# Whole expert tiles as pairs of 64-row half products, ordered by a one-word ScalarE copy

## The chip, the cores and the metric

The kernel runs on one core of a Trainium2 chip. The metric is device time in microseconds (us) of one execution. The core's engines run instruction streams of their own and meet only at semaphores: TensorE (PE: matmuls, and PEld: its weight loads), VectorE (DVE), ScalarE (ACT), GpSimd (POOL) and SyncE (SP), which issues most DMAs. SBUF is the on-chip memory with 128 partitions; PSUM holds TensorE's sums, in eight banks of 512 32-bit numbers a partition.

## The reference

Two stages. First an attention without softmax, for 8 batches of 2496 tokens, 256 channels and 64 key channels; then a mixture of 8 experts, of which each token takes the best one.

```python
scores = np.matmul(z, z.transpose(0, 2, 1)) / S
attn = np.maximum(scores, 0.0) ** 2
x = (u * np.matmul(attn, v)).reshape(N, D)            # N = 19968, D = 256

logits = x @ w_gate + modality_bias[modality_id]
e_idx = np.argmax(logits, axis=1)                     # E = 8
gate_w = softmax(logits)[arange(N), e_idx]
for e in range(E):
    mask = e_idx == e
    h = np.maximum(x[mask] @ w1[e], 0.0)              # F = 1024
    out[mask] = gate_w[mask, None] * (h @ w2[e])
```

## The kernel before, in words

All products use fp32r operands. To keep the precision, each operand is split into a high part and a low part, and a product is the sum of three: high by high, high by low, low by high.

The attention stage works through steps of two key tiles (2 x 128 rows) against 512 (in the last chunk 448) queries. Its contraction over 64 channels, and its weighing by key rows, are laid out as products on 64 rows of the array: rows 0-63 and rows 64-127 hold two different ones, which run side by side and write to different banks (`scores`, L279; `weigh`, L334). ACT squares and rounds, DVE makes low parts. At the end of a chunk the output is turned into rows of tokens by transposes on TensorE (`make_rows` L412; for the very last chunk `make_last_rows` L394) and multiplied by u (`take_rows`, `take_last_rows` L403); DVE makes the gate's logits (L434), and POOL scatters the tokens into one DRAM list per expert (L547).

The expert stage takes tiles of T = 512 tokens of one expert. Four "early" tiles, t = -4 to -1, belong to the expert with the most tokens and start before routing is complete; in between their steps the rest of the logits, the routing and the plan of all later tiles are made (lists `between[n][f]`, run after step f of the n-th tile). Tiles 0 to 34 follow the plan, so 39 tiles are whole. What is left over goes through `run_quarter` and, under conditions read at run time, further tiles.

For one whole tile `run_tile` goes through f = 0 to 7, one slice of 128 of the 1024 hidden channels each:

- `up(t, f)`: six products of 128 x 128 weights and 512 tokens add into one bank of `ps_h` (four banks, tag "h"): 2 halves of the contraction over 256 channels, 3 terms each. ACT then writes `hh` = relu of the bank, rounded (L1009), and DVE the low part `hl` (L1010).
- `down(t, f - 2, ...)` for each of J = 4 groups of 128 tokens: one product of `hh` with the high and low parts of w2 side by side (512 columns, L1018) and one of `hl` with the high part (256 columns, L1019). They add into four banks of `ps_o`, one for each group, over all eight f.
- After the last step `finish` scales by the gate: ACT takes one half of the bank (L1033), DVE adds the other (L1035), and POOL scatters the rows to the output with an indirect DMA (L1037).

Beside the products, for the next tile: `part_weights_high` / `part_weights_low` split its weights into high parts (ACT, L831) and low parts (DVE, L835), in four quarters at f = 2 to 5; `turn_blocks` transposes its tokens (DVE, L853) at f = 6, and `part_high` (ACT, L860) and `part_low` (DVE, L865) split them at f = 7. `fetch_weights(t + 2)` issues two DMAs of 1 MB on SP's queue (L811, L815) at the start of a tile, into one of three weight buffers; `prefetch` issues the DMAs of tokens (L792).

In this stage the order on PE, ACT, DVE, POOL and SP is the order in which the program issues the instructions (`manual_schedule`); every engine works its queue in order.

## Time and profile before

| | |
|---|---|
| median of 3 runs | 2243.7 us (2242.93 to 2245.5) |
| profiled execution, its own time | 2245.74 us |
| its span, first to last instruction | 2243.9 us |
| mean granted TensorE clock | 0.997 |
| PE busy | 2221.6 us, 99% of the span |
| DVE busy | 1804.4 us, 80% |
| ACT busy | 1573.0 us, 70% |
| up products of 512 columns (L1005) | 1872 of 128 x 128 weights |
| down products, 512 / 256 columns (L1018 / L1019) | 1256 / 1256 |

An engine's busy time counts its own instructions, without waits. In the timelines below, each row is one instruction or a run of like ones: start, length, engine, line, operation, output and inputs by their names in the program, rows x columns of the weights, shape of the moving operand, count, and in brackets the idle time before it with what ended it. TensorE's products overlap: the next one starts before the last has ended, so the cost of one in a stream is the distance from start to start. A product's end is modelled from its start.

### The profile page before, as it was taken

The numbers are of one execution on the slowest core, as the hardware profiler recorded it, in microseconds if no ns is written. First come the engines' busy times: TensorE is split into PE (matmuls) and PEld (weight loads), VectorE is DVE, ScalarE is ACT, GpSimd is POOL, SyncE is SP. The second block draws the span as 40 slices with busy tenths as digits, with TensorE's granted clock in tenths as the row PEclk, the third lists the DMA queues.
The fourth block names the chain that finished last, engine by engine and source line by source line (L and its number), as shares of the span: only waits on it lengthen the run. The fifth ranks groups of instructions, "written<-read, shape, count | busy, mean of one in ns | idle before, by whom it ended". The sixth has DMA issues, their size and how long they took to land.

```text
span 2243.9 us, 44470 instructions
## 1 busy us (share of the span) xinstructions
PE 2221.6 (99%) x16874; PEld 2020.7 (90%) x16874; DVE 1804.4 (80%) x4552; ACT 1573.0 (70%) x1917; POOL 366.3 (16%) x349
## 2 busy tenths in 40 slices
PE   9999999999999999999999999999999999999996
PEld 7889999999999999999999888888888888888885
DVE  7889989989989989989989998666666666666663
ACT  7888888888888888888888873455555555555452
POOL 0000220220210210220220422211111111111111
PEclk9999999999999999999999999999999999999998
DMA  5222223222012112112111122754545454545440
GB/s 184 111 70 101 83 89 110 79 74 79 32 59 75 35 57 76 35 56 75 39 45 40 51 88 62 187 158 126 157 128 155 127 155 130 152 134 149 135 140 23
DMA packets 199602, 216.64 MB, mean 97 GB/s; under 512 B 118448, under 2 KB 166064, under 8 KB 194512
## 3 DMA queue, kind: packets, MB, share of 16 engines
q1 hardware_dynamic: 184288, 172.49, 26.3%
q0 software_dynamic: 15088, 41.21, 5.0%
q8 instruction: 134, 2.20, 0.4%
q14 instruction: 92, 0.75, 0.1%
HBM read 168.23 MB, written 62.19 MB: 103 GB/s over the span
## 4 chain that ended last, share of the span: by engine, by line
PE 59%; issue 25%; DMA 9%; POOL 3%; DVE 3%; ACT 1%; POOLq 0%; DVEq 0%; ACTq 0%
PE acc L334 44%; PE s L279 12%; DMA out_dram<-y,ids 9%; POOL out_dram L1037 3%; DVE spare L434 1%; PE ph L1005 1%; PE po L412 1%; PE po L1018 1%; DVE al L318 1%; PE po L1019 0%; DVE vl L249 0%; POOLq L1037 0%; PE warm L886 0%; DVE ah L309 0%; DVE x L382 0%
## 5 line engine op out<-in xcount | busy, mean ns | idle before, releaser
L287 ACT ACTIVATE r<-s 128x1024 f32<-128x1024 f32 (+1 forms) x395 | 397.8, 1007 | 184.5 <-PE s L279 182.7
L318 DVE TENSOR_TENSOR al<-r,ah 128x1024 fp32r<-128x1024 f32 (+1 forms) x359 | 429.8, 1197 | 84.1 <-ACT ah L309 68.9
L334 PE MATMUL acc<-ah,vh 64*128 64x512 f32 (+1 forms) x3120 | 492.8, 383 | 1.0 <-DVE ah L301 1.0
L334 PE MATMUL acc<-ah,vl 64*128 64x512 f32 (+1 forms) x3120 | 487.0, 382 | 0.0
L334 PE MATMUL acc<-al,vh 64*128 64x512 f32 (+1 forms) x3120 | 483.8, 381 | 0.0
L434 DVE SCALAR_TENSOR_TENSOR spare<-x,wgb 128x256 f32<-128x256 f32 x1280 | 462.4, 421 | 1.0
L1009 ACT ACTIVATE hh<-ph 128x512 fp32r<-128x512 f32 x312 | 186.6, 598 | 388.2 <-PE ph L1005 348.1
L1018 PE MATMUL po<-w,hh 128*128 128x512 f32 x1256 | 450.0, 394 | 0.0
L1005 PE MATMUL ph<-xh,w 128*128 128x512 f32 x1248 | 430.1, 395 | 1.4 <-DVE x L382 1.4
L293 ACT ACTIVATE r<-r 128x1024 f32<-128x1024 f32 (+1 forms) x399 | 415.6, 1042 | 3.5
L334 PEld LDWEIGHTS acc<-ah,vh 64*128 64x128 f32 x3120 | 383.3, 184 | 17.7 <-ACT x L378 1.7
L334 PEld LDWEIGHTS acc<-al,vh 64*128 64x128 f32 x3120 | 383.0, 184 | 14.6
L334 PEld LDWEIGHTS acc<-ah,vl 64*128 64x128 f32 x3120 | 381.3, 184 | 15.0 <-DVE vl L249 0.2
L1010 DVE SCALAR_TENSOR_TENSOR hl<-ph,hh 128x512 fp32r<-128x512 f32 x312 | 215.7, 691 | 219.5 <-ACT hh L1009 191.8
L279 PE MATMUL s<-zm 64*128 64x512 f32 (+1 forms) x2400 | 388.8, 386 | 0.8 <-ACT r L287 0.3
L547 POOL DMA_INDIRECT xs<-x,sloti x160 | 206.5, 1291 | 1016.2 <-DVE x L545 971.9
L1019 PE MATMUL po<-w,hl 128*128 128x256 f32 x1256 | 351.5, 280 | 0.2 <-DVE hl L1010 0.2
L279 PEld LDWEIGHTS s<-zm 64*128 64x128 f32 x2400 | 292.6, 185 | 12.3 <-ACT r L287 0.8
L309 ACT CAST ah<-r 128x1024 fp32r<-128x1024 f32 (+1 forms) x283 | 288.1, 1018 | 0.0
L1005 PEld LDWEIGHTS ph<-xh,w 128*128 128x128 f32 x1248 | 234.2, 188 | 57.6 <-DVE x L382 1.8
L1018 PEld LDWEIGHTS po<-w,hh 128*128 128x128 f32 x1256 | 235.7, 188 | 55.4
L1037 POOL DMA_INDIRECT out_dram<-y,ids x157 | 152.8, 974 | 693.7 <-DVE y L1035 659.2
(155 smaller groups left out, 1979.4 us busy)
## 6 DMA issues: line engine op xcount, KB each, us to landing
w<-w1s SPq DMA_DIRECT2D x37, 1024.0 KB
w<-w2s SPq DMA_DIRECT2D x37, 1024.0 KB
xg<-xs SPq DMA_DIRECT2D x156, 128.0 KB
vr<-in_v_dram SPq DMA_DIRECT2D x32, 512.0 KB
ut<-in_u_dram SPq DMA_DIRECT2D x32, 512.0 KB
zr<-in_zt_dram SPq DMA_DIRECT2D x40, 256.0 KB
w1s<-in_moe_w_dram SPq DMA_DIRECT2D x16, 512.0 KB
w2s<-in_moe_w_dram SPq DMA_DIRECT2D x8, 1024.0 KB
```

What stands on the lines that cost most here:

```text
L279: nc.tensor.matmul(out=s[t][:, :w], lhsT=lhs, rhs=mv[halves[t], ql, :w], start=n == 0, stop=n == 2)
L287: nc.scalar.activation(out=r[:, :, :w], in_=both[:, :, :w], func=AF.Relu, scale=INV)
L293: nc.scalar.square(out=a[:, :, :w], in_=a[:, :, :w])
L309: copy(out=ah[:, :, :w], in_=st_a[g][:, :, :w])
L318: nc.vector.tensor_tensor(out=al[:, :, :w], in0=a[:, :, :w], in1=ah[:, :, :w].bitcast(F32), op=ALU.subtract)
L334: nc.tensor.matmul(out=acc[b, c][r][dh][:, :w], lhsT=V[b, k // J][y][halves[r], k % J, dh * P:(dh + 1) * P], rhs=x[halves[r], k % 2, :w], ...
L434: nc.vector.scalar_tensor_tensor(out=spare[:, k % 2, :], in0=x[:, j, 0:D], scalar=1.0, in1=wgb[:, e, :], op0=ALU.mult, op1=ALU.mult, accum ...
L1005: nc.tensor.matmul(out=ph, lhsT=lhs, rhs=rhs[:, k, :], start=n == 0, stop=n == 3 * KD - 1)
L1010: nc.vector.scalar_tensor_tensor(out=hl, in0=ph, scalar=0.0, in1=hh.bitcast(F32), op0=ALU.max, op1=ALU.subtract)
L1018: nc.tensor.matmul(out=po[j], lhsT=hh[:, s], rhs=both, start=f == 0, stop=False, skip_group_check=True)
L1019: nc.tensor.matmul(out=po[j][:, 0:D], lhsT=hl[:, s], rhs=w[:, 0, :], start=False, stop=f == KF - 1, skip_group_check=True)
L1037: nc.gpsimd.indirect_dma_start(out=out, out_offset=bass.IndirectOffsetOnAxis(ap=ids[:, j:j + 1], axis=0), in_=y, in_offset=None, bounds_ch ...
```

## The change

Whole tiles are run by a new `run_whole`. `run_tile` stays for what is under conditions.

- A product over all 128 rows becomes two half products: rows 0-63 and rows 64-127 of the same operands. They are issued in pairs: rows 0-63 for one slice beside rows 64-127 for its neighbour (direction d = 0), and in a later pass the other way round (d = 1). In `up_half` the two slices are two slices of hidden channels with a bank of `ps_h` each; in `down_half` they are two groups of 128 tokens with a bank of `ps_o` each.
- Thus each bank gets the sums of one row half first and those of the other later. `product` notes which half wrote a bank last (`writer`). Where it was the other half, the product is made to wait for the ScalarE copy held in `ended["act"]`. `change` issues such a copy, of one word of SBUF, which waits for the last product issued before it, and makes it the one held.
- Order in a tile: `UPS` gives for each of eight steps the pair of slices and the direction of the up pass; `DOWNS` the slices and the direction of a down pass behind it. Two down passes of a tile, `last_but_one` (slices 4 to 7, d = 1) and `last` (slices 6 and 7, d = 0, and `finish`), go to the list `behind` and are run in the first two steps of the next tile.
- The quarters of the next tile's weights are split at steps 0 (two), 3 and 7, `turn_blocks` moves to step 5, `part_high` and `part_low` to step 6, and `fetch_weights(t + 2)` to the end of step 1.
- The last chunk's rows of the attention stage are turned by `make_rows` (16 half transposes in place of 8 whole ones), into two banks of `ps_o`, at step 0 of the first tile.

```diff
@@ -993,6 +975,13 @@
     for n in range(1, NW):
         weight_tiles(wp, n)
 
+    def rectify(ph, nt):
+        hh = mp.tile([P, T], F32R, tag="hh", bufs=4, name="hh")[:, 0:nt]
+        hl = mp.tile([P, T], F32R, tag="hl", bufs=4, name="hl")[:, 0:nt]
+        nc.scalar.activation(out=hh, in_=ph, func=AF.Relu)
+        nc.vector.scalar_tensor_tensor(out=hl, in0=ph, scalar=0.0, in1=hh.bitcast(F32), op0=ALU.max, op1=ALU.subtract)
+        return hh, hl
+
     def up(t, f):
         _, xh, xl = TL[t]
         w = weights_of(t)[0]
@@ -1004,11 +993,53 @@
             for lhs, rhs in ((wh, xh), (wh, xl), (wl, xh)):
                 nc.tensor.matmul(out=ph, lhsT=lhs, rhs=rhs[:, k, :], start=n == 0, stop=n == 3 * KD - 1)
                 n += 1
-        hh = mp.tile([P, T], F32R, tag="hh", bufs=4, name="hh")[:, 0:nt]
-        hl = mp.tile([P, T], F32R, tag="hl", bufs=4, name="hl")[:, 0:nt]
-        nc.scalar.activation(out=hh, in_=ph, func=AF.Relu)
-        nc.vector.scalar_tensor_tensor(out=hl, in0=ph, scalar=0.0, in1=hh.bitcast(F32), op0=ALU.max, op1=ALU.subtract)
-        return hh, hl
+        return rectify(ph, nt)
+
+
+
+
+    ended = {"pe": None, "act": None}
+    writer = {}
+
+    def product(out, lhs, rhs, r, key, start, stop):
+        m = ins_of(nc.tensor.matmul(out=out, lhsT=lhs, rhs=rhs, start=start, stop=stop, skip_group_check=True))
+        if writer.get(key, r) != r:
+            tc.add_manual_dep(m, ended["act"].name, data, reason="the other half's sums")
+        writer[key] = r
+        ended["pe"] = m
+
+    def change():
+        i = ins_of(nc.scalar.copy(out=one_of[:, 0:1], in_=one_of[:, 1:2]))
+        tc.add_manual_dep(i, ended["pe"].name, data, reason="products of one half")
+        ended["act"] = i
+
+    def up_half(t, g, d, banks):
+
+        _, xh, xl = TL[t]
+        w = weights_of(t)[0]
+        terms = [(k, q, x) for k in range(KD) for q, x in ((0, xh), (0, xl), (1, xh))]
+        for n, (k, q, x) in enumerate(terms):
+            for r, rows_of in enumerate(halves):
+                i = (r + d) % 2
+                c = slice((g + i) * P, (g + i + 1) * P)
+                product(
+                    banks[i], w[rows_of, q, k, c], x[rows_of, k, :], r, (t, "h", g + i),
+                    n == 0 and not d, n == len(terms) - 1 and d == 1,
+                )
+
+    def down_half(t, fs, h, po, d):
+
+        for p in range(0, J, 2):
+            for f in fs:
+                hh, hl = h[f]
+                w = weights_of(t)[1][:, f]
+                for x, y in ((hh, w.rearrange("p h d -> p (h d)")), (hl, w[:, 0, :])):
+                    for r, rows_of in enumerate(halves):
+                        i = p + (r + d) % 2
+                        product(
+                            po[i][:, 0:y.shape[1]], x[rows_of, i * P:(i + 1) * P], y[rows_of], r, (t, "o", i),
+                            f == 0 and not d and x is hh, f == KF - 1 and not d and x is hl,
+                        )
 
     def down(t, f, h, po, j):
         hh, hl = h
@@ -1084,41 +1115,86 @@
             down(t, f, h[f], po, 0)
         finish(t, po, f"out{t}{part}")
 
-    def turn_at(t):
-        return 4 if t == 1 - EARLY else KF - 2
-
-    def run_tile(t, ahead, extra={}, part=""):
+    def run_tile(t, part=""):
+
         if len(TL[t]) < 3:
             turn(t)
         po = [ps_o.tile([P, 2 * D], F32, tag="o", name="po") for _ in range(TL[t][0].shape[1])]
         h = {}
-        for f in range(KF + 2):
-            if f < KF:
-                h[f] = up(t, f)
-            if 2 <= f < KF:
+        for f in range(KF):
+            h[f] = up(t, f)
+            if f >= 2:
                 for j in range(len(po)):
                     down(t, f - 2, h[f - 2], po, j)
-            if ahead and t >= -1 and 2 <= f < 2 + KD + 2:
-                part_weights_high(t + 1, f - 2)
-                part_weights_low(t + 1, f - 2)
-            for g in extra.get(f, ()):
-                g()
-            if ahead and t + 1 in TL:
-                if f == turn_at(t):
-                    turn_blocks(t + 1)
-                if f == turn_at(t) + 1:
-                    part_high(t + 1)
-                    part_low(t + 1)
         for j in range(len(po)):
             for f in range(KF - 2, KF):
                 down(t, f, h[f], po, j)
         finish(t, po, f"out{t}{part}")
 
+    assert KF == 8 and J == 4
+    UPS = [(0, 0), (0, 1), (2, 0), (4, 0), (2, 1), (4, 1), (6, 0), (6, 1)]
+    DOWNS = {3: ((0, 1), 0), 4: ((0, 1), 1), 5: ((2, 3), 0), 6: ((2, 3), 1), 7: ((4, 5), 0)}
+    behind = []
+
+    def run_whole(t, ahead, extra={}):
+
+        if len(TL[t]) < 3:
+            turn(t)
+        po, h, banks = [], {}, {}
+        for f, (g, d) in enumerate(UPS):
+            if not d:
+                banks[g] = [ps_h.tile([P, T], F32, tag="h", name="ph") for _ in halves]
+            up_half(t, g, d, banks[g])
+            if d:
+                h.update({g + i: rectify(x, T) for i, x in enumerate(banks.pop(g))})
+            elif f != 2:
+                change()
+            parts = {0: (0, 1), 3: (2,), 7: (3,)}.get(f, ()) if ahead and t >= -1 else ()
+            if f < KF - 1:
+                for q in parts:
+                    part_weights_high(t + 1, q)
+                    part_weights_low(t + 1, q)
+            if ahead and f == 6:
+                part_high(t + 1)
+                part_low(t + 1)
+            if behind and f < 2:
+                behind.pop(0)()
+            if f == 1 and t >= 0 and t + 2 < min(UNC + 1, MAXT):
+                fetch_weights(t + 2)
+            if f in DOWNS:
+                if not po:
+                    po += [ps_o.tile([P, 2 * D], F32, tag="o", name="po") for _ in range(J)]
+                fs, d = DOWNS[f]
+                down_half(t, fs, h, po, d)
+                change()
+            if f == KF - 1:
+                for q in parts:
+                    part_weights_high(t + 1, q)
+                    part_weights_low(t + 1, q)
+            for e in extra.get(f, ()):
+                e()
+            if ahead and f == 5:
+                turn_blocks(t + 1)
+
+        def last_but_one():
+            down_half(t, (4, 5, 6, 7), h, po, 1)
+            change()
+
+        def last():
+            down_half(t, (6, 7), h, po, 0)
+            finish(t, po, f"out{t}")
+
+        behind[:] = [last_but_one, last]
+        if t == UNC - 1:
+            while behind:
+                behind.pop(0)()
+
 
     assert EARLY > 3
     between = {n: {f: [] for f in range(KF + 2)} for n in range(EARLY)}
-    between[0][1] += [lambda: make_last_rows(B - 1, NCH - 1)]
-    between[0][2] += [lambda: take_last_rows(B - 1, NCH - 1)]
+    last_rows = [ps_o.tile([P, J, KD, DK], F32, tag="o", name="po") for _ in halves]
+    between[0][0] += [lambda: make_rows(B - 1, NCH - 1, last_rows)]
+    between[0][1] += [lambda: [take_rows(B - 1, NCH - 1, r) for r in range(2)]]
     slots = [(n, f) for n in range(EARLY) for f in range(KF)]
 
     def put(slot, *pieces):
@@ -1146,11 +1222,9 @@
         prefetch(t)
         if t == 0:
             assert next(planning, planning) is planning
-        if t >= 0 and t + 2 < min(UNC + 1, MAXT):
-            fetch_weights(t + 2)
         if t == UNC - 1 and MAXT > UNC:
             fetch(UNC, 0, 1)
-        run_tile(t, t + 1 < min(UNC + 1, MAXT), between.get(t + EARLY, {}))
+        run_whole(t, t + 1 < min(UNC + 1, MAXT), between.get(t + EARLY, {}))
 
     if MAXT > UNC:
 
@@ -1171,7 +1245,7 @@
                     if r == 1:
                         run_quarter(t, "b")
                     else:
-                        run_tile(t, False, part="ac"[r // 2])
+                        run_tile(t, part="ac"[r // 2])
 
 
 _INS = ["u", "v", "zt", "moe_modality_id", "moe_w_gate", "moe_modality_bias", "moe_w1", "moe_w2"]
```

21 lines of the change are left out of this document (3 added, 18 removed).

## Prediction

> **What bounds the kernel now.** I read the page first, then the busy time by stretch, then TensorE's timeline in both stages.
>
> ```profile
> span 2243.9 us, 44470 instructions
> PE 2221.6 (99%) x16874; PEld 2020.7 (90%) x16874; DVE 1804.4 (80%) x4552; ACT 1573.0 (70%) x1917; POOL 366.3 (16%) x349
> PEclk9999999999999999999999999999999999999998
> ```
>
> TensorE (PE) is busy for 99% of the span at full clock; nothing else is near. The last 40% of the span is the expert stage, which the change rewrites:
>
> ```profile
> core 0: us, PE busy (x) PEld busy (x) DVE busy (x) ACT busy (x) POOL busy (x), PEclk, DMA share, GB/s
> 1400.00:2200.00 800.00, 800.00 (x4006) 672.69 (x4005) 528.91 (x702) 404.14 (x606) 148.42 (x152) 1.00 0.50 143
> ```
>
> PE has no idle time at all there. A whole tile is 48 up products, 32 down products of 512 columns and 32 of 256, 112 in all, so it takes 800 / 4006 x 112 = 22.37 us, and ScalarE (ACT) is half idle. The 39 whole tiles (t = -4 to 34) make 872 us. What an up and a down step cost, from PE's timeline:
>
> ```profile
> 1600.32 0.40 PE L1005 MATMUL ph<-xh,w 128*128 128x512 f32 x1
> 1600.55 0.39 PE L1005 MATMUL ph<-xl,w 128*128 128x512 f32 x1
> ...
> 1601.71 0.40 PE L1018 MATMUL po<-w,hh 128*128 128x512 f32 x1
> 1601.94 0.28 PE L1019 MATMUL po<-w,hl 128*128 128x256 f32 x1
> 1602.06 0.39 PE L1018 MATMUL po<-w,hh 128*128 128x512 f32 x1
> ...
> 1603.12 0.40 PE L1005 MATMUL ph<-xh,w 128*128 128x512 f32 x1
> ```
>
> The first column is the start. Six up products take 1601.71 - 1600.32 = 1.39 us, 0.232 each; the down products 0.23 and 0.12. So only two things can move the time: what a product costs, and any wait that PE is given. The second column is a product's own length from start to result, 0.40 or 0.28 us; in the stream most of it overlaps the next one, in a wait it doesn't.
>
> **The change, part by part.**
>
> *The products.* Each full product becomes one half-row product on each of two slices, running side by side on rows 0-63 and 64-127: as many pairs as there were products. The attention stage already runs such pairs (PE's timeline again; the last column counts half products):
>
> ```profile
> 20.37 0.96 PE L279 MATMUL s<-zm 64*128 64x512 f32 x6 [0.34 <-ACT r L287]
> 21.17 1.08 PE L334 MATMUL acc<-ah,vh 64*128 64x512 f32 x8
> ...
> 23.90 0.84 PE L279 MATMUL s<-zm 64*128 64x512 f32 x6
> 653.66 1.11 PE L334 MATMUL acc<-ah,vh 64*128 64x448 f32 x8
> ...
> 656.70 1.11 PE L334 MATMUL acc<-ah,vh 64*128 64x448 f32 x8
> ```
>
> Twelve pairs of 512 columns take 23.90 - 21.17 = 2.73 us, 0.2275 a pair; fifteen of 448 take 3.04, 0.203. The three pairs from 20.37 had to wait for ACT, and with nothing to hide their first weight load they take 0.80 instead of 0.68 us: a load not hidden costs 0.12, of which I count 0.11. A pair of 512 costs 0.0045 less than the full product's 0.232. Pairs of 256 columns aren't in the trace. Carried down from 512 and 448 along a line (0.0245 for 64 columns) one would be 0.130; like the full product (2.06 less 1.94), 0.117 to 0.12; and no less than a weight load, 0.11. I take 0.117, since the full product of the same width is the nearest row. A tile's products then take 80 x 0.2275 + 32 x 0.117 = 21.94 us: 0.43 less, times 39 is **-17 us**, with ends of -25 (at 0.110) and 0 (at 0.130).
>
> *The order.* The two halves of a slice add into one bank, so the code puts a ScalarE copy between them. `change` lets the copy wait for the last product issued so far; `product`, where the other half wrote the bank before, waits for `ended["act"]`, which is the latest copy issued, not the one that followed that bank's last product. I write U for a half of an up step, D for a half of a down step, | for a copy. A tile on PE is: U00 | L1 of the tile before | U01, L2 of the tile before, U20, U40 | D01a | U21, D01b | U41, D23a | U60 | D23b | U61, D45a |. Every swapped bank does have another piece of work between its halves. But a copy stands at the end of that piece too, and the next swapped product waits for that one. The first product right behind the copy is a swapped one six times a tile: L1, U01, U21, U41, D23b, U61. There PE drains. (D01a and U20, U40, U60, U00 write fresh banks; L2, D01b, D23a, D45a wait for a copy already waited for.) Each drain is built from these rows, first groups by line and shape (count, busy us, mean ns of one, idle before), then three of the timeline:
>
> ```profile
> L1018 PE MATMUL po<-w,hh 128*128 128x512 f32 x1256 | 450.0, 394 | 0.0
> L1019 PE MATMUL po<-w,hl 128*128 128x256 f32 x1256 | 351.5, 280 | 0.2 <-DVE hl L1010 0.2
> L243 ACT CAST vh<-vr 128x1024 fp32r<-128x1024 f32 x39 | 40.6, 1041 | 0.0
> L229 ACT CAST zm<-zr 128x512 fp32r<-128x512 f32 x40 | 24.7, 618 | 1.4 <-DMA zr<-in_zt_dram 1.4
> L860 ACT CAST xh<-xt 128x256 fp32r<-128x256 f32 x1 | 0.4, 398 | 0.0
> L473 ACT ACTIVATE ex<-sh 128x64 f32<-128x64 f32 x1 | 0.2, 243 | 0.0
> 2223.71 0.28 PE L1072 MATMUL ph<-xh,w 128*128 128x128 f32 x1
> 2224.03 0.60 ACT L1078 ACTIVATE hh<-ph 128x512 fp32r<-128x512 f32 x1 [1.99 <-PE ph L1072]
> 19.30 1.02 ACT L287 ACTIVATE r<-s 128x1024 f32<-128x1024 f32 x1
> ```
>
> 1. The last product ends 0.28 us after its start (0.39 for an up piece).
> 2. PE to ACT: the product of 2223.71 ends at 2223.99, ACT starts at 2224.03: 0.04.
> 3. The copy. ACT's SBUF casts fall from 1041 ns at 1024 elements to 618 at 512 and 398 at 256, 0.83 ns an element, which leaves 0.19 us for one element. Upper bound: the 64-element row, 0.243. Lower: 0.12, an estimate that a third of that fixed part is saved on one partition; no row shows an ACT instruction that small.
> 4. ACT to PE: the relu ends at 20.32, PE starts at 20.37: 0.05.
> 5. The weight load that the wait holds back: 0.11, as above.
>
> After a down piece: 0.28 + 0.04 + 0.19 + 0.05 + 0.11 = 0.67 us to the next product, where it would have been 0.12: 0.55 lost. After an up piece 0.78 against 0.23: the same. With the copy's bounds a drain costs 0.48 to 0.60. Tiles: 5 drains in the first (no tile before it, so U01 stands behind U00's copy and L1 is missing), 6 in each of 38, and 2 when the last tile's L1 and L2 follow its end: 235. **+129 us**, ends +113 and +141.
>
> *Is ACT free when a copy comes?* The work queued ahead of it, by length:
>
> ```profile
> L1009 ACT ACTIVATE hh<-ph 128x512 fp32r<-128x512 f32 x312 | 186.6, 598 | 388.2 <-PE ph L1005 348.1 <-issue 35.1 <-DVE p_last L670 4.9
> L831 ACT CAST w<-w 128x1024 fp32r<-128x1024 f32 x148 | 154.0, 1042 | 0.0
> ```
>
> Ahead of the copy after L1 (2.8 us of products) stand two weight casts, 2.08 us. Ahead of those after D01b and D23a (1.38 us) stand two relus, 1.20. Ahead of those after D01a and D23b stands one cast of 1.04. All fit, so I add nothing. What queues behind a waiting copy on ACT (casts, `part_high`) has a piece of PE work to itself. The one-slot margins are about 0.2 us, though; were each relu pair late by 0.2, that is 2 x 0.2 x 39 = 16 us more, which I put into the upper end.
>
> *Moved steps.* `fetch_weights` (two DMAs on SP's queue) goes from the tile's start to after L2 of the tile before, some 8 us later (U00, L1, U01 and L2 are 36 pairs and two drains). Nothing behind it on SP is due before the next tile. The transfer is short beside a tile:
>
> ```profile
> 1613.78 0.37 SPq L811 DMA_DIRECT2D w<-w1s  x1
> ...
> 1622.00:1624.00 2.00, 2.00 (x12) 1.69 (x11) 1.62 (x2) 1.04 (x2) 0.00 (x0) 1.00 0.37 137
> 1624.00:1626.00 2.00, 2.00 (x13) 1.70 (x12) 1.12 (x3) 1.54 (x2) 0.00 (x0) 1.00 0.00 0
> ```
>
> Issued at 1613.8, all traffic is over before 1624: under 10 us. The casts that need it come a tile later, 25 - 8 + 1.5 = 18 us after the issue: cost nothing. The casts, `turn_blocks` and the split of x move within a tile, off the path. The first tile is different: VectorE (DVE) is full there.
>
> ```profile
> 1326.00:1349.00 23.00, 21.62 (x190) 19.05 (x187) 22.00 (x71) 13.86 (x18) 5.12 (x6) 1.00 0.11 39
> 1349.00:1371.00 22.00, 21.77 (x109) 18.07 (x109) 20.25 (x73) 7.02 (x12) 1.65 (x2) 1.00 0.46 79
> ```
>
> DVE works 20 to 22 us of 22 (logits). The change needs the low parts of h after some 3 us instead of 5.6, and ACT's `part_high` now waits for `turn_blocks`, queued behind four logits, with a copy behind it. I take +3 us, between 0 and 8. The last rows' transposes (16 halves for 8) change some 0.5 us either way, within that.
>
> **Sum:** -17 + 129 + 3 = +115 us. Against the profiled execution's own 2245.7 us that is 2360.7; the median of the runs, 2243.7, lies 2.0 below, so **2359 us**, 5.1% slower. Its own range: 2243.7 - 25 + 113 + 0 = 2332 to 2243.7 + 0 + 141 + 8 + 16 = 2409.
>
> The Trainium skill ("TensorE: Matmul & The Clock Gate", Part 3, The mechanism) says that a weight load overlaps matmuls in flight only where its row group differs. Here the full products at 1600.32 and 1600.55 follow at 0.23 us with all rows in use, where a load that was not hidden would add 0.11; the trace does not agree. By that rule each half would pay its own load, 0.11 x 112 x 39 = +480 us, which the pairs from 21.17 do not show either.
>
> **The rivals.**
>
> *The drain does not happen (faster).* If the wait were met in time, because the copy waited for is an older one, the place is the six swaps, and the price zero: 2243.7 - 17 + 3 = 2230. It decides below 14 / 235 = 0.06 us per drain. For it: every bank does have a piece of 1.4 to 2.8 us between its halves, so a wait tied to that bank would be covered. Against: `ended["act"]` is read when the product is issued, and 20.37 shows PE standing until ACT ends. 8%. That products and drains just cancel, within 0.2% (4.5 us, about what a measurement of this kernel can tell): 3%.
>
> *Loads of 256-column pairs do not run side by side.* Then such a pair needs two loads, 0.22: 0.10 x 32 x 39 = +128 us more, 2487. Against: the 128-column loads of the attention stage's pairs fit into 0.2275 with room for two only just, so it isn't excluded; but the release at 20.37 cost one load for two halves. 5%, and the page's rule above, which goes further, lies in these.
>
> *The clock.* Six gaps of 0.3 us a tile might lower the granted clock; at half speed the products' 856 us would double, 3215 us in all. Against, at the start of the kernel:
>
> ```profile
> 10.00:16.00 6.00, 5.54 (x46) 3.82 (x44) 4.55 (x7) 5.36 (x7) 0.00 (x0) 1.00 0.94 369
> ```
>
> PE idle 8% of that stretch, clock 1.00. 2%. The same page of the Trainium skill (Part 1) has the clock halved after an idle window of about 3.4 us; these gaps are a tenth of that, and by that rule nothing is lost.
>
> **How the numbers follow.** The forecast case has 82%, the rivals 8, 3, 5 and 2. The range 2328 to 2412 takes the forecast's own ends and a few us; what it leaves out is the faster, the cancelling and the two costlier cases, 18%. Faster 0.08, same 0.03, slower 0.89.
>
> **What would show it.** Right: the expert stage's tile at 25.2 us, PE busy about 93% there, ACT copies of 0.19 us, nine a tile, and six idle gaps of about 0.3 us a tile, put down to ACT's copy; half pairs of 512 at 0.2275. Wrong: swapped products that follow without a gap; a copy far from 0.19; pairs of 256 columns at 0.13 or 0.22; gaps put down to DVE or a DMA; a clock under 1.

## The result and the profile after

The changed kernel took 2428.6 us (median of 4 runs, 2427.3 to 2430.5) beside 2244.6 us for the kernel before on the same chip: 1.0821 times as long, 95% interval 1.0803 to 1.084, 184 us more. The forecast was 2359, between 2328 and 2412: the direction held, the size did not. From the page of the changed kernel:

```profile
span 2426.4 us, 53916 instructions
PE 2291.2 (94%) x21250; PEld 2020.9 (83%) x21250; DVE 1780.5 (73%) x4552; ACT 1617.4 (67%) x2268; POOL 365.3 (15%) x349
PEclk9999999999999999999999999999999999999998
```

TensorE fell from 99% of the span to 94%, at full clock nearly everywhere: 135 us of the span are now idle (2426.4 - 2291.2), where 22 were. In the stretch of steady expert tiles (columns as in the prediction's tables by stretch) and in the waits of TensorE in that stretch (us in total, times, longest):

```profile
1500.00:2200.00 700.00, 630.83 (x5884) 488.78 (x5882) 368.65 (x498) 328.05 (x683) 103.20 (x106) 1.00 0.42 120
```

```profile
PE ph L1005 <- ACT c_most L1012: 51.5, 106, 0.9
PE po L1005 <- ACT c_most L1012: 17.7, 52, 0.3
```

158 waits, all for the one-word copy, 69.2 us together. Each tile ends with one cast of its token ids, so the first and the last start of that cast give the length of a tile: (2189.3 - 1523.3) / 25 = 26.64 us in the changed kernel, (2194.8 - 1501.1) / 31 = 22.38 before. 700 / 26.64 is 26.3 tiles, so the waits are six a tile, as forecast; the forecast tile was 25.2 us. The two rows (the tile with ids, the kernel before first):

```profile
L1028 DVE CAST ids<-gate x32: 162/163/164, 1501.1 to 2194.8; 128x4 int32<-128x4 f32 x32
```

```profile
L1059 DVE CAST ids<-gate x26: 157/158/163, 1523.3 to 2189.3; 128x4 int32<-128x4 f32 x26
```

**An ordinary drain**, in the timeline of the changed kernel:

```profile
1702.21 0.40 PE L1005 MATMUL ph<-xh,w 64*128 64x512 f32 x2
1702.70 0.19 ACT L1012 COPY c_most<-c_most 1x1 f32<-1x1 f32 x1 [0.26 <-PE ph L1005]
1702.95 0.50 PE L1005 MATMUL po<-w,hh 64*128 64x512 f32 x2 [0.34 <-ACT c_most L1012]
1703.28 0.28 PE L1005 MATMUL po<-w,hl 64*128 64x256 f32 x2
1703.40 0.39 PE L1005 MATMUL po<-w,hh 64*128 64x512 f32 x2
...
1705.71 0.28 PE L1005 MATMUL po<-w,hl 64*128 64x256 f32 x2
1706.08 0.19 ACT L1012 COPY c_most<-c_most 1x1 f32<-1x1 f32 x1 [1.28 <-PE po L1005]
1706.33 0.50 PE L1005 MATMUL ph<-xh,w 64*128 64x512 f32 x2 [0.34 <-ACT c_most L1012]
```

The last pair before the wait starts at 1702.21 and ends 0.40 later; the copy starts at 1702.70, 0.09 after that end, takes 0.19, and TensorE starts at 1702.95, 0.06 after it. That is 0.74 us where a pair takes 0.23, so 0.51 lost; the pair after the wait needs 0.33 to the next one (1703.28) instead of 0.23: its weights are loaded only from 1702.94 on, so this load is not hidden. Together 0.61 a drain.

**The drain after D01a is longer**, in nearly every tile:

```profile
1713.25 0.97 POOL L1068 DMA_INDIRECT out_dram<-y,ids  x1 [0.30 <-issue]
1713.32 0.28 PE L1005 MATMUL po<-w,hl 64*128 64x256 f32 x2
1714.23 0.19 ACT L1012 COPY c_most<-c_most 1x1 f32<-1x1 f32 x1 [0.86 <-PE po L1005]
1714.47 0.50 PE L1005 MATMUL ph<-xh,w 64*128 64x512 f32 x2 [0.87 <-ACT c_most L1012]
```

Here the pair ends at 1713.60 and the idle ScalarE begins the copy at 1714.23, 0.63 later instead of 0.09. The row above is one of the four scatters with which GpSimd writes a finished tile's rows (line 1068); it had begun 0.35 us before the pair ended, and here the copy starts as it ends.

**The start of the expert stage**: the first half product runs at 1342.12, and its partner, which writes a second bank, waits. The granted clock behind it (seventh column) is about half (0.5 from 1344.5 to 1351.3, 6.8 us):

```profile
1342.12 0.39 PE L1005 MATMUL ph<-xh,w 64*128 64x512 f32 x1
1346.40 0.79 PE L1005 MATMUL ph<-xh,w 64*128 64x512 f32 x1 [3.88 <-DVE x L382]
```

```profile
1344.00:1351.00 7.00, 4.60 (x33) 4.13 (x35) 2.42 (x6) 0.19 (x1) 0.97 (x1) 0.53 0.13 38
```

### The profile page after: what moved, and what is told of

It reads as the page before. It is cut to its first block, busy times and chain, and to the rows that moved or that the text cites. A ratio compares the mean times of both kernels' runs of the same rounds, so it can differ in the third digit from the quotient of the medians.

```text
span 2426.4 us, 53916 instructions
## 1 busy us (share of the span) xinstructions
PE 2291.2 (94%) x21250; PEld 2020.9 (83%) x21250; DVE 1780.5 (73%) x4552; ACT 1617.4 (67%) x2268; POOL 365.3 (15%) x349
## 4 chain that ended last, share of the span: by engine, by line
PE 91%; ACT 3%; DVE 3%; issue 2%; DMA 0%; another core or an unknown queue 0%; POOL 0%; ACTq 0%; SPq 0%; DVEq 0%; POOLq 0%
PE acc L334 40%; PE po L1005 19%; PE ph L1005 19%; PE s L279 11%; ACT c_most L1012 2%; PE po L394 1%; DVE spare L416 1%; DVE al L318 0%; POOL out_dram L1068 0%; DVE vl L249 0%; ACTq L1012 0%; PE warm L868 0%; DVE xt L835 0%; DVE ah L309 0%
## 5 line engine op out<-in xcount | busy, mean ns | idle before, releaser
L1005 PE MATMUL ph<-xh,w 64*128 64x512 f32 x2496 | 457.4, 407 | 86.9 <-ACT c_most L1012 77.4
L1005 PE MATMUL po<-w,hh 64*128 64x512 f32 x2496 | 459.7, 399 | 26.9 <-ACT c_most L1012 26.5
L982 DVE SCALAR_TENSOR_TENSOR hl<-ph,hh 128x512 fp32r<-128x512 f32 x312 | 200.9, 686 | 343.4 <-ACT hh L981 343.3
L1005 PEld LDWEIGHTS ph<-xh,w 64*128 64x128 f32 x2496 | 237.8, 185 | 186.8 <-ACT c_most L1012 125.7
L981 ACT ACTIVATE hh<-ph 128x512 fp32r<-128x512 f32 x312 | 169.7, 596 | 287.9 <-PE ph L1005 275.6
L1005 PE MATMUL po<-w,hl 64*128 64x256 f32 x2496 | 350.9, 278 | 0.0
L1005 PEld LDWEIGHTS po<-w,hh 64*128 64x128 f32 x2496 | 235.0, 184 | 114.1 <-ACT c_most L1012 60.5
```

Of the source, the lines that this page charges most:

```text
L981: nc.scalar.activation(out=hh, in_=ph, func=AF.Relu)
L982: nc.vector.scalar_tensor_tensor(out=hl, in0=ph, scalar=0.0, in1=hh.bitcast(F32), op0=ALU.max, op1=ALU.subtract)
L1005: m = ins_of(nc.tensor.matmul(out=out, lhsT=lhs, rhs=rhs, start=start, stop=stop, skip_group_check=True))
```

## The experiments

Six groups, each with its kernels put on a chip anew and beside its own runs of the kernel before (2244.4 to 2245.7 us, so that one is the same in all). "Loading" below is one such group; the times above are of a seventh.

**1. The drains.** e1 lets each swapped product wait for the copy behind its own bank's last product:

```
-            tc.add_manual_dep(m, ended["act"].name, data, reason="the other half's sums")
+            tc.add_manual_dep(m, own[key].name, data, reason="the other half's sums")
...
     def change():
...
+        own.update({key: i for key in since})
+        since.clear()
```

> Each swapped product waits for the copy that followed its own bank's last product, not for the latest copy; all products, copies and their order stay. Drain theory: the six gaps a tile vanish, because a piece of 1.4 to 2.8 us lies between; a tile falls from 26.66 to the sum of its pairs, 80 x 0.232 + 32 x 0.1165 = 22.3 us, and the time to 2243 to 2256 us (the upper end if the first four tiles keep the 13 us that they lost). Rival, half products or copies cost by themselves: a tile stays above 25 us and the time above 2380. If the 0.56 us by which the down pass of step 3 ends late is a delay of TensorE's work itself and not only of its signal, a tile comes to 22.85 and the time to 2265 to 2278.

2264.5 us (1.0085, 1.0068 to 1.0102). By stretch:

```profile
1500.00:2200.00 700.00, 700.00 (x6996) 587.40 (x6994) 439.36 (x596) 389.81 (x813) 124.33 (x128) 1.00 0.50 142
```

TensorE has no idle time at all, with nine copies a tile still there: in the steady tiles the copies cost nothing, and the waits for the latest copy are what costs. A tile is 22.41 us, as in the drain theory; the time is 8 us above the theory's upper end, all of it lost in the first tiles (e2, next). The 164 us from here to the changed kernel are not all drains: the changed kernel's loading has late signals (below) and this one has none.

e2 keeps the order and computes each product over all 128 rows, with no copies:

```
-            for r, rows_of in enumerate(halves):
-                i = (r + d) % 2
...
+            nc.tensor.matmul(out=banks[d], lhsT=w[:, q, k, c], rhs=x[:, k, :], start=n == 0, stop=n == len(terms) - 1)
```

> The changed order of pieces with products over all 128 rows and no copies. If the order alone costs nothing in a steady tile: 22.37 us a tile, and what the time stands above 2244 is what the first four tiles lose by the order (0 to 13 us): 2244 to 2257. Rival, the order itself costs (late low parts, late weights): above 2300 us.

2254.9 us (1.0043, 1.0027 to 1.006). By stretch:

```profile
1500.00:2200.00 700.00, 700.00 (x3499) 588.15 (x3499) 442.75 (x593) 349.20 (x531) 126.13 (x124) 1.00 0.49 140
```

3499 full products in 700 us, and in e1 6996 half products, 3498 pairs, in the same 700 us. A pair and a full product take the same time. The 9.6 us between e1 and e2, on one loading, are lost in the first tiles: the sixth tile's cast of token ids starts at 1500.0 in e1 and at 1490.4 in e2.

e3 lets only the up halves wait for their own copy, so that two drains a tile are left (L1 and D23b):

```
+            tc.add_manual_dep(m, (own[key] if key[1] == "h" else ended["act"]).name, data, reason="the other half's sums")
```

> Only the up passes wait for their own bank's copy; the down passes still wait for the latest one. Drain theory: four of the six gaps a tile go, two of 0.61 us stay (before the last-but-one pass and before the down pass of step 6): 2 x 0.61 x 39 = 48 us above the kernel in which all six go, 2290 to 2305. Rival, a cost per copy or per pair: within 10 us of the changed kernel's 2428.

2309.4 us (1.0282, 1.0265 to 1.03), 4 us above the theory's range.

```profile
L1063 DVE CAST ids<-gate x30: 159/160/163, 1505.6 to 2191.6; 128x4 int32<-128x4 f32 x30
```

(2191.6 - 1505.6) / 29 = 23.66 us a tile: 1.25 over e1's 22.41 for two drains, 0.62 each. Six at that price would be 3.75; the changed kernel has 26.64 - 22.41 = 4.23. The rest is the long one.

e4 issues the scatters later in GpSimd's program:

```
-            i = ins_of(nc.gpsimd.indirect_dma_start(...
+            rows_out.append((ids[:, j:j + 1], y))
...
+        if late:
+            later.append(send)
```

> The changed kernel with the four scatters of a tile's rows issued after step 4 of the next tile, not in step 1. If the scatters make the down pass of step 3 end 0.56 us late, that delay goes from its place, 39 x 0.56 = 22 us less, 2405 to 2410, or turns up at a later drain instead, then no change. If they have nothing to do with it: 2426 to 2431, with the delay at the same place.

2398.0 us (1.0678, 1.0661 to 1.0696), tile 26.07, no long drain: less than either theory said. But GpSimd had not been held back: its scatters still start as soon as y is there, as before. So e4 says that the lateness can be absent with the scatters in place, not why. In hindsight it is the loading (end of this section): no kernel of this group has it, though e1, e3 and e4 too end pieces 0.35 to 0.4 us into a scatter.

**2. The scatters.** e5 is the changed kernel unedited.

> The changed kernel once more, unedited. In the first profile of it, the ordering copy after D01a began 0.6 to 0.7 us after its last product's recorded end, in every whole tile with a tile before it, against 0.1 us at the other five drains. Theory: this belongs to the kernel (its order of instructions fixes how the drain stands to other work), so it is here again: steady tile 26.6 to 26.7 us, time 2427 to 2430 us. Rival: it belongs to that chip or that loading of the program: tile 26.06 us as with the scatters written later, time about 2405 us.

2445.6 us (1.0892, 1.0874 to 1.091): 17 us more than the same kernel had at first, which neither theory held.

```profile
L1059 DVE CAST ids<-gate x25: 158/160/161, 1523.5 to 2175.0; 128x4 int32<-128x4 f32 x25
```

(2175.0 - 1523.5) / 24 = 27.15 us a tile. The place is the same, after D01a, only longer: up to 1.7 us of idle time.

e6 leaves the scatters out:

```
+            if t < UNC - 1:
+                continue
             i = ins_of(
                 nc.gpsimd.indirect_dma_start(
```

> The changed kernel without the scatters of finished rows (GpSimd's indirect DMAs at the end of a tile) for all whole tiles but the last; everything else as it was, so most rows of the output are not written. Theory: the late release after D01a comes from the scatter that GpSimd is issuing at that moment: without scatters the tile falls to 26.06 us (22.41 + 6 x 0.608), some 22 us less in all, about 2405 us. Rival 1: the scatters have nothing to do with it: 26.6 to 26.7 us, 2427 us. Rival 2: the scatters cost TensorE something at every drain: tile under 25.9 us.

2394.6 us (1.0671, 1.0653 to 1.0689), 51 us under e5 on the same chip. Tile, then TensorE's waits in 1500 to 2200:

```profile
L1059 DVE CAST ids<-gate x27: 157/159/163, 1513.8 to 2191.7; 128x4 int32<-128x4 f32 x27
```

```profile
PE ph L1005 <- ACT c_most L1012: 37.0, 108, 0.6
PE po L1005 <- ACT c_most L1012: 18.4, 54, 0.3
```

26.07 us a tile, 22.41 + 6 x 0.61, and 162 waits of 0.34 us on average. The tile is the theory's, the time 10 us under its figure. The long drain needs the scatters.

e7 holds the four scatters until the copy after D01b:

```
+                if t < UNC - 1:
+                    tc.add_manual_dep(i, ended["act"].name, data, reason="a later start")
```

> The changed kernel, with each finished tile's four scatters held until the copy after D01b, so that GpSimd issues them some 4 us later. Theory: a drain whose last product ends while GpSimd issues a scatter gets its release late; D01a's then comes at once (0.1 us) and the lateness moves to U41's or D23b's drain, if one falls into a scatter in the same way; tile 26.06 us if none does, 26.6 if one does. Rival: the lateness belongs to D01a itself (its banks, its products): it stays there, tile 26.6 to 26.7 us.

2468.9 us (1.1004, 1.0985 to 1.1022), the slowest of all; (2192.9 - 1500.0) / 25 = 27.72 us a tile, more than either forecast. The timeline:

```profile
1623.24 0.40 PE L1005 MATMUL ph<-xh,w 64*128 64x512 f32 x2
1623.26 0.98 POOL L1075 DMA_INDIRECT out_dram<-y,ids  x1 [0.30 <-DMA out_dram<-y,ids]
1625.28 0.19 ACT L1012 COPY c_most<-c_most 1x1 f32<-1x1 f32 x1 [2.75 <-remote]
1625.52 0.50 PE L1005 MATMUL po<-w,hh 64*128 64x512 f32 x2 [1.89 <-ACT c_most L1012]
```

Now D01a's drain is ordinary, and the one after U60, which meets the fourth scatter, waits 1.89 us: its pair ends at 1623.64, its copy comes at 1625.28, 1.04 us after the scatter itself is over. (The semaphore that this copy waits for is TensorE's; the view says "remote" because the signal came over 1.5 us after the pair's end.) The lateness goes where the scatter goes. (I had named U41 or D23b as its next place; it was D23b.)

e8 gives the first tile full rows, in the own-copy kernel:

```
+            if t == -EARLY:
+                c = slice((g + d) * P, (g + d + 1) * P)
+                nc.tensor.matmul(out=banks[d], lhsT=w[:, q, k, c], rhs=x[:, k, :], start=n == 0, stop=n == len(terms) - 1)
+                continue
```

> The kernel whose swapped products wait for their own copy (2264.5 us), but with the first whole tile's products over all 128 rows, without copies. With own copies the start of the expert stage showed TensorE idle for 3.9 us and then a granted clock of 0.5 for 6.8 us; with full rows throughout the idle time was 2.5 us and the clock stayed at 1.00 there (2254.9 us). Theory: the first pair needs two free banks at once, and the idle time that this makes halves the clock: here the first tile is back at some 22.5 us, no 0.5 behind the start, time 2257 to 2260 us. Rival: the 9.6 us come from the copies in ScalarE's queue in all four early tiles: time 2262 to 2264 us and the early tiles still at 25 to 26 us.

2279.6 us (1.0156, 1.0139 to 1.0173). This missed both: on this loading the own-copy order loses time in the steady tiles too (22.9 us instead of 22.41), so its time can't be set against e1's. Its start can: the idle time fell to 2.52 us, and the clock still went to half for about 3.4 us (0.76 over 7 us), which it had not done in e2 after 2.53 us. In e13 below, the kernel of e2 once more, it did after 2.51 us (0.76 over the same 7 us).

```profile
1346.13 0.71 PE L394 MATMUL po<-ident,x 64*128 64x64 f32 x16 [2.52 <-DVE x L382]
```

```profile
1345.00:1352.00 7.00, 5.87 (x32) 4.71 (x33) 3.81 (x9) 1.18 (x2) 0.97 (x1) 0.76 0.25 60
```

**3. Controls for the scatters.** e9 and e10 leave the scatters out in the same way, of the kernel before and of the own-copy kernel; e12 is the own-copy kernel unedited.

> The kernel before without the scatters of finished rows for all whole tiles but the last (most rows of the output are not written): the control for the same edit on the changed kernel, which gave 2394.6 us against 2445.6 with scatters on that chip. Theory: with full-row products and no drains TensorE stands for no scatter, so nothing is saved: 2241 to 2246 us, tile 22.37 us. Rival: the scatters cost the kernel before as much as the changed one, and the 51 us say nothing of the change: about 2195 to 2220 us.

2241.2 us (0.998, 0.9971 to 0.999): 4.5 us less. The scatters cost the kernel before a tenth of what they cost the changed one.

> Half-row pairs whose swapped products wait for their own bank's copy, and no scatters of finished rows for all whole tiles but the last. Theory: what that kernel was slower than before by (19 us, nearly all in the first tiles) is mostly scatters as well; without them the first tiles cost some 3 us, as they did in the changed kernel without scatters: 2248 to 2253 us, steady tile 22.41 us. Rival: the first pair's wait for two banks and the halved clock make the 19 us: 2260 to 2264 us.

2256.9 us (1.0051, 1.0034 to 1.0068), between the two forecasts: the scatters make part of that kernel's excess (19.4 us against e12 below). Against e9, the kernel before without the same scatters, 15.7 us are left: 10 are the price of the changed order (e13 below), the rest fits that of half rows in the first tiles.

e11 writes the same rows from SyncE's queue:

```
+            if t < UNC - 1:
+                r0 = (t + EARLY) * T + j * P
+                nc.sync.dma_start(out=out[r0:r0 + P, :], in_=y)
+                continue
```

> The changed kernel with the finished rows of all whole tiles but the last written by plain transfers from SyncE's queue, to consecutive rows instead of their own: the same bytes from the same tiles at the same place of the program, without GpSimd and its descriptors. Theory: it is GpSimd's issue of a scatter that holds TensorE or its release: tile 26.06 us as without any scatter, 2394 to 2398 us. Rival: it is the writing of the rows itself: tile 26.6 us or more, 2420 to 2446 us.

2395.5 us (1.0669, 1.0651 to 1.0687), as without any scatter. It is GpSimd's scatter, not the writing of the same bytes. Whether its issue or its transfers hold the signal, e11 doesn't tell, since it takes both away.

> The own-copy kernel once more, unedited (2264.5 us, steady tile 22.41, no idle time in the steady tiles). Theory: how much the scatters hold TensorE differs between loadings of a program, as it did for the changed kernel (2428.6 and 2445.6), so this may come anywhere from 2264 to 2280 us, with gaps of 0.3 us beside the fourth scatter where it is slow. Rival: the own-copy order is free of it and only the first full-row tile made the difference: 2264 to 2266 us again.

2276.3 us (1.0135, 1.0118 to 1.0152), where e1, the same kernel, took 2264.5. Its timeline shows the lateness without a drain:

```profile
1620.56 0.97 POOL L1072 DMA_INDIRECT out_dram<-y,ids  x1 [0.30 <-issue]
1620.64 0.40 PE L1005 MATMUL ph<-xh,w 64*128 64x512 f32 x2
1620.88 0.39 PE L1005 MATMUL po<-w,hh 64*128 64x512 f32 x2
1621.10 0.28 PE L1005 MATMUL po<-w,hl 64*128 64x256 f32 x2
...
1622.42 1.09 ACT L981 ACTIVATE hh<-ph 128x512 fp32r<-128x512 f32 x2 [1.94 <-PE ph L1005]
```

U21's last pair ends at 1621.04 and TensorE goes straight on, 0.23 us a pair. But the relu that reads this result starts at 1622.42, 1.38 us after that end, with ScalarE idle. TensorE's stream is not held up: the signal that the products are done is late. The trace has the time of that signal too, the update of TensorE's semaphore: 1622.40, and the relu starts 0.02 after it, so ScalarE loses nothing. Since a product's end is modelled, whether only the signal was late or the last sums too is not shown.

**4. Halves or drains.** e13 is e2 again, e14 the own-copy kernel a third time, and e15 is e2 with the copies and with the six waits a tile of the changed kernel, though nothing needs them:

```
+            if d and not n:
+                tc.add_manual_dep(m, ended["act"].name, data, reason="the other half's sums")
```

> The changed order with full-row products and no copies once more, unedited (2254.9 us the first time, steady tile 22.41 us), beside the next two on one chip. Theory: without drains and with full rows TensorE stands for no scatter on any loading: 2253 to 2257 us, steady tile 22.41. Rival: the changed order alone is enough: steady tiles over 22.5 us and a time over 2260, as the own-copy kernel has here.

> The own-copy kernel (half-row pairs, no drains) for a third time, as the measure of this loading: 2264 us with steady tiles of 22.41, or up to 2280 us with tiles of 22.65 to 22.9, as it had been on the first and on the later loading. It decides between no theories by itself; the kernels beside it are read against it.

> The changed order with full-row products, and with the copies and the six waits per tile of the changed kernel (the first product of the second unit of each pair waits for the latest copy, though nothing needs it). Scatters as in the kernel before. Theory A: the half-row pairs, twice as many instructions for TensorE, are what a scatter can hold up: with full rows a tile is 26.06 us (22.41 + 6 x 0.608) and the time about 2395 to 2405 us. Theory B: a drain that ends inside a scatter is released late whatever the products are: tile 26.6 to 27.4 us, time 2425 to 2446 us.

e13 2255.1 us (1.0045, 1.0028 to 1.0062), e14 2275.1 (1.0133, 1.0116 to 1.015), e15 2393.4 (1.0665, 1.0647 to 1.0682). Tiles of e14 and e15:

```profile
L1063 DVE CAST ids<-gate x31: 157/159/162, 1502.4 to 2182.1; 128x4 int32<-128x4 f32 x31
```

```profile
L1045 DVE CAST ids<-gate x27: 157/160/160, 1509.3 to 2186.0; 128x4 int32<-128x4 f32 x27
```

On one chip, half rows without drains lose 0.25 us a tile (22.66) and full rows none (22.41 in e13), and full rows with drains have 26.03 us with the scatters in place. So in steady tiles late signals came with half rows and not with drains. But the pieces of e13 end 0.65 to 0.9 us into a scatter and those of e15 0.8 to 0.95 (up pieces of the kernel before 0.7 to 0.95), the late ones of e14 0.35 to 0.5: the rows and the moment are not told apart yet.

**5. Rows or moment.** e16 (e15) and e17 (the changed kernel) put 0 to 8 memsets of 0.15 us ahead of a tile's first scatter, so that the drains meet the scatters at every moment; e18, alone on a sixth loading, does it with nine tiles of half rows and nine of full rows in turn:

```
+            if not j and t < UNC - 1:
+                for _ in range((t + EARLY) % 9):
+                    m = ins_of(nc.gpsimd.memset(spare_words, 0.0))
+                    tc.add_manual_dep(m, i.name, data, reason="a later start")
```

> Full-row products with the copies and the six waits a tile (2393.4 us), and ahead of each tile's first scatter 0 to 8 small memsets on GpSimd (tile number modulo 9) that wait for the first finished row: the scatters start 0 to some 1.3 us later, so that the drain after D01a ends at every moment of a scatter in turn. Before, it ended 0.8 to 0.9 us into one; the late signals of the half-row kernels fell 0.3 to 0.5 us into one. Theory A (half rows): no copy comes late at any moment, 0.1 us behind the last product throughout, tile 26.03 us in every step. Theory B (the moment): copies come 0.5 to 1.6 us late in the steps in which the drain ends 0.3 to 0.5 us into a scatter, 2 or 3 tiles in 9.

> The changed kernel (half rows) with the same memsets, so the same sweep of its scatters against its drains. Theory A: late at some or all moments of a scatter, and this beside a full-row kernel on the same chip that is not. Theory B: late only where the drain ends 0.3 to 0.5 us into a scatter, as in the full-row kernel beside it; in the other steps the tile is 26.07 us.

> The swept kernel with nine tiles of half rows, nine of full rows, and so on, so that both kinds meet the scatters at the same moments on one loading. On the loading of the last two runs neither kind was late at any moment (2395.7 and 2403.0 us), so this tells the two apart only where the loading has late signals. Then theory A (half rows): copies come 0.5 to 1.6 us late in half-row tiles alone. Theory B (the moment): in both kinds, where a drain ends 0.3 to 0.5 us into a scatter. With no late signals at all: about 2398 us, and it stays open.

2395.7, 2403.0 and 2404.1 us (1.0668, 1.0701, 1.0707; each within 0.0032 either way), and no long drain in any. TensorE's waits in e17:

```profile
PE ph L1005 <- ACT c_most L1012: 36.7, 107, 0.6
PE po L1005 <- ACT c_most L1012: 18.4, 54, 0.3
```

They are those of e6, which had no scatters at all (37.0 and 18.4). On these two loadings half rows and full rows are alike, at all moments, so these three don't decide the question. They do give the price of half rows without late signals: e17 takes 7.3 us more than e16, on one loading.

**What the traces of all runs say of the loading and the rows.** Up to its last chunk the attention stage is the same in all kernels, and GpSimd scatters there too (the tokens into their lists). One place of it, in the changed kernel and in e1:

```profile
249.46 0.94 PE L279 MATMUL s<-zm 64*128 64x512 f32 x5
249.56 1.24 POOL L529 DMA_INDIRECT xs<-x,sloti  x1 [0.30 <-issue]
251.02 1.03 ACT L287 ACTIVATE r<-s 128x1024 f32<-128x1024 f32 x1 [1.37 <-PE s L279]
```

```profile
249.47 0.94 PE L279 MATMUL s<-zm 64*128 64x512 f32 x5
249.57 1.23 POOL L529 DMA_INDIRECT xs<-x,sloti  x1 [0.30 <-issue]
250.45 1.03 ACT L287 ACTIVATE r<-s 128x1024 f32<-128x1024 f32 x1 [0.79 <-PE s L279]
```

The scores end at 250.40 and 250.41; ScalarE starts 0.62 us after that in the one and 0.04 in the other. Counted by the updates of TensorE's semaphore that come over 0.25 us after their product's end, before 1300 us: 19 to 22 in each of the 13 traces of the kernel before, the changed kernel and e5 to e15, none in the seven of e1 to e4 and e16 to e18. So the lateness belongs to the loading and meets every kernel on it, the kernel before too, which loses no time by it (2244.4 to 2245.7 us on all loadings). It is not the chip alone: e9 to e12 and e18 ran on the same one. And e4, e16, e17 and e18, on loadings without it, say nothing about rows.

Half rows are not needed for it. e15, with full rows, near its end:

```profile
2369.21 0.98 POOL L1054 DMA_INDIRECT out_dram<-y,ids  x1 [0.30 <-issue]
2369.80 0.27 PE L1089 MATMUL ph<-xh,w 128*128 128x128 f32 x1
2371.05 0.60 ACT L1095 ACTIVATE hh<-ph 128x512 fp32r<-128x512 f32 x1 [3.03 <-PE ph L1089]
```

The full product ends at 2370.07, and the relu, which waits for it alone, starts 0.98 us later; a relu is 1.0 late in the same way at 2232.87 in e13 and 0.7 at 1420.83 in the kernel before. In the steady tiles the moment matters: in the changed kernel the pieces that end some 0.2 us into a scatter are signalled in time, and those 0.35 us into one late, tile after tile. The full products of steady tiles (the kernel before, e13, e15) end 0.45 to 0.95 us into one and are in time, while the half-row ones of e14 at 0.45 to 0.5 were late, so the rows may still bear on which moments are bad. What makes a moment a bad one is open.

## Why the prediction was wrong

The runs split the 184 us by pairs of kernels: the order, e13 less before, 2255.1 - 2245.2 = +9.9; the drains, e15 less e13, 2393.4 - 2255.1 = +138.3; half rows without late signals, e4 less e15, 2398.0 - 2393.4 = +4.6 (on one loading each, e17 less e16 has +7.3 and e1 less e2, copies included, +9.6, so 5 to 10); late signals, the changed kernel less e4, 2428.6 - 2398.0 = +30.6, on the loading of e5 +47.6. Together 183.4. The last two differences go across loadings, on which the kernel before moved by 1.3 us, and e4 issues its scatters at another place of the program.

**Drains, +129 predicted, +138 measured: right in cause, places and count.** Copies of 0.19 us, six waits a tile. The step that was short is "PE to ACT", 0.04: it is 0.09. ACT has a separate semaphore instruction ahead of the copy that the relu, from which I took 0.04, doesn't have; from TensorE's signal to the copy are 0.08 us (1625.20 to 1625.28 in e7), to a relu 0.02 (e12). The ends of 113 to 141 hold it. ACT was free in time, as costed (0 of the 16 us upper end).

**Products, -17 predicted, 0 measured: a step that failed is "a pair of 512 costs 0.0045 less than the full product".** The attention stage's 0.2275 was carried to a stage in which the full product takes 0.232; there the pair takes 0.232 too. e1 against e2 shows it: 3498 pairs and 3499 products in 700 us. What makes the expert stage's 0.232 is open; it does not change with the rows.

**First tiles, +3 predicted (0 to 8), about +10 measured for the order, and 5 to 10 more for the half rows.** The bound was too low. By stretch, the kernel before and e2:

```profile
1345.00:1460.00 115.00, 114.04 (x575) 96.04 (x576) 90.77 (x249) 45.60 (x75) 31.97 (x32) 1.00 0.49 126
```

```profile
1345.00:1460.00 115.00, 109.29 (x543) 90.60 (x544) 85.17 (x241) 41.12 (x68) 29.53 (x29) 0.99 0.47 120
```

5.7 us of TensorE's time are idle there instead of 1.0, waiting for VectorE's low parts, ScalarE's high parts and, at the start, for banks that the first tile now needs earlier; the rest of the 10 I did not resolve. With half rows the first pair needs two banks at once: 3.88 us of idle time, and half clock behind it, neither of which the step held. The Trainium skill ("TensorE: Matmul & The Clock Gate", Part 1, What's actually happening) puts the halving down to an activity window of some 3.4 us that runs free of the kernel. The 3.4 us of half clock after 2.52 us of idle time in e8 and 2.51 in e13, and none after 2.53 in e2, the same kernel as e13, agree with a free-running window, and show that a gap shorter than the window can be enough.

**What no step held: late signals, 31 to 48 us.** This is the step that took the time out of the range: the sum has no term for GpSimd's scatters and gives no reason for leaving it out; GpSimd, 16% busy, falls under "nothing else is near". Its scatters are still on no path, but at some moments of one, a piece's end reached ScalarE 0.5 to 1.6 us late, and the drain waits for that signal. Shown are, on the loadings that have it: the scatters are needed (e6 beside e5), it is GpSimd's scatter and not the bytes (e11), the place follows the scatter (e7), TensorE itself runs on (e12), and neither the half rows nor the drains are needed for a late signal (the kernel before, e13). With half rows it costs 31 to 48 us with drains and some 12 without (e12 less e1). Not shown: what differs between loadings, which moments are bad and why. The Trainium skill ("DMA: Bandwidth & Descriptors", SWDGE vs HWDGE vs iDMA) says that GpSimd appends the descriptors of its transfers to rings in SBUF. e11, where GpSimd doesn't issue the finished rows' transfers, has no lateness in these tiles; whether those writes hold the signal, no run here shows.

Of the rivals, none came: the drains happened, the 256-column pairs take 0.12 us (from 1703.28 to the next start at 1703.40 in the changed kernel's timeline), and the clock in the steady tiles stayed at 1.00. Without late signals the time would have been inside the range, at 2398 us (e4), but 39 us over the forecast: products, first tiles and drains were all off to the same side.

## What to carry to other kernels

Let a product wait for the event that covers its hazard, not for the latest one issued: the same copies cost next to nothing or 138 us by which of them is waited for, since one trip from TensorE over ScalarE and back is 0.61 us. Splitting a product that already fills the rows bought nothing; take an instruction's price from the stage that is changed, not from another. An engine that is 16% busy can still delay another one's signals, and where it does, it may do so on one loading of the program and not on the next, so repeat a kernel before explaining a difference of 1%.

## What the runs showed of the hardware that I had not expected

- The end of a product reached ScalarE late when it fell into a GpSimd scatter: up to 1.6 us for a half-row pair (1623.64 to 1625.28 in e7), 0.98 for a full product (e15), with TensorE's own stream running on (1620.88 and 1621.10 in e12).
- All traces on four of the seven loadings have this, none on the other three.
- The same kernel took 2428.6 us on one loading and 2445.6 on another, the own-copy kernel 2264.5, 2276.3 and 2275.1; the kernel before stayed within 2244.4 to 2245.7 throughout.
- Products of 512 columns take 0.232 us in the expert stage, with full and with half rows, and pairs 0.2275 in the attention stage. Whether ScalarE and VectorE are busy makes next to no difference (0.2322 to 0.2333 on average in the kernel before, 1500 to 2200, by which of them is busy for most of the product); the cause is open.
- 2.52 us of idle time halved TensorE's clock for about 3.4 us (e8); 2.51 and 2.53 us in two executions of one kernel did so once (e13) and once not (e2).
